# Attention, gated product and token mixing on one core: Newton steps of 1/sqrt and their transfers moved to GpSimd, stores of the w_out results issued by ScalarE, normalization moved behind the last gate, first attention by pairs of heads

## The chip, the core and the metric

One core of one Trainium2 chip runs the whole program. The core has TensorE (PE; its weight loads are shown as PEld), VectorE (DVE), ScalarE (ACT), GpSimd (POOL) and SyncE (SP), each with a queue of its own that it works off in order, and sixteen DMA engines which the queues of SP, ACT and POOL feed. The metric is the device time of the program in microseconds: 755.64 is the median of three runs of the kernel before.

## The reference, cut to what matters

```python
kv  = einsum('bhsd,bhse->bhde', k, v)              # 8 batches, 8 heads, 576 tokens, 64 wide
out = einsum('bhsd,bhde->bhse', q, kv)
x   = out / sqrt(mean(out * out, -1) + 1e-6) * g_norm   # per token and head, then heads side by side: 512 channels
g   = sigmoid(causal 5-tap convolution of x over the tokens, per channel)
x   = (g * (x @ w_val)) @ w_out                    # ends the first stage
theta = x @ w_theta                                # second stage
u   = x + w_tok_r @ (x * cos(theta)) + w_tok_i @ (x * sin(theta))
out = u + max(u @ w_ch, 0)
```

## The kernel before

Channels lie on the partitions, in four blocks of 128 (`m`), the 576 tokens on the free axis in two halves of 288. Every product with a weight is made of three fp32r matmuls (high times high, high times low part, low times high), so each operand is split: ScalarE rounds it (`xh`, `gh`, `wvh`, `woh`; L68), VectorE subtracts (`xl`, `gl`, ...; L69).

**First stage, per batch.** `key_value` makes keys times values for the 8 heads (TensorE, tile `kvp`; ScalarE copies it to `kvs`). `attention` makes four groups `o` of two heads' halves; of each, ScalarE takes the square (`sq`, L204) and a scaled copy into `x` (L205). Then 32 small matmuls (`ss`, L212) sum the squares; VectorE adds epsilon and makes 1/sqrt by an integer first guess and three Newton steps on 128x72 (L219 to L225, tiles `ss`, `hm`, `t`, `y`). For batches 2 to 7 `y` goes to DRAM (`rd`, L228) and comes back spread over all partitions (`yb`, L233), on SyncE's queue; for batches 0 and 1 TensorE spreads it by matmuls with `sel` into PSUM (`yb`, L254). `normalize` multiplies `x` by it (L246 from the transfer, L257 from PSUM) and splits `x`. `conv` makes the gate `acc`: ScalarE starts it (L263), VectorE adds four taps (L265), ScalarE takes the sigmoid (L266). `value` makes x times w_val for the four blocks (`v`); VectorE multiplies by the gate (L288, called the gate below) and the result is split into `gh` and `gl`. `first` makes the product with w_out (`y_0` to `y_3`): three quarters of y_0 and y_1, their last quarters (which need the fourth `gl`), then y_2 and y_3; ScalarE copies them (`yo`) and SyncE's queue stores them to DRAM (L305).

**The order.** The main loop over the batches is software pipelined: while batch i is in `value` and `first`, batch i+2 has its `key_value` and `attention`, and batch i+1 is normalized. All of a program's instructions are put on the engines' queues by a list scheduler, by priority in the order of the code and its own estimates, so code that moves is interleaved anew. `tc.issue_after(ins)` queues what a block puts on the engine of `ins` behind it. All products of the first stage share four PSUM slots of two banks (`pd`): `kvp`, `o`, `ss`, `yb`, `v` and `y` in turn, so a tile may wait until the tile before it in its slot has been read.

Weights come as 64 bit words and are decoded in four VectorE steps and one ScalarE step per chunk (`decode`), then split. The list START (L31) is the order of the first loads: v0 to v3 are chunks of w_val, o0 to o3 of w_out, k0 to k7 and q0 to q7 pairs of heads of batches 0 and 1, c0 the convolution. Decode of the second stage's weights (`todo`, `toks`; L429 to L440) is put behind the normalization of batches 1 to 6 at low priority.

**Second stage**: theta, the token mix `u` and the channel product `c`, batch after batch; the diff does not touch it.

Of the kernel before, what the change touches and what calls it, by code (L numbers as in the profile page):

```python
# [43 lines left out]
def attention_moe_holo_kernel(ctx, tc, kvm, kvt, qt, gn, w_val, conv_w, w_out, w_th, w_tok, w_ch, outT):  # L44
# [126 lines left out]
    def key_value(b, kv):  # L171

        ps = one_bank(f"kvp{b}")
        for g in range(2):
# [9 lines left out]
        kvs_of[b] = pa.tile([P, NP, D], F32, tag="kvs", bufs=2, name=f"kvs{b}")  # L184
        nc.scalar.activation(kvs_of[b], ps[:, 0:NP * D].rearrange("p (a e) -> p a e", e=D), AF.Copy)

    def attention(b, q):
# [5 lines left out]
        for h in range(2):  # L193
            sl = slice(h * HS, (h + 1) * HS)
            for g in range(2):
                o = two_banks(f"o{b}_{h}_{g}")
                for e in range(2):
                    for j in range(2):
                        rows = slice(j * D, (j + 1) * D)
                        mm = nc.tensor.matmul(o[e * D:(e + 1) * D, j, :], kv[rows, 2 * g + e, :], q[g][rows, e, sl],  # L200
                                              start=True, stop=True, tile_position=(j * D, e * D))
                ch = slice(2 * g, 2 * g + 2)
                sq[h, g] = px.tile([P, 2, HS], F32, tag="sq", bufs=4, name=f"sq{b}_{h}_{g}")
                nc.scalar.activation(sq[h, g], o, AF.Square, scale=0.125)  # L204
                nc.scalar.activation(x[:, ch, PAD + h * HS:PAD + (h + 1) * HS], o, AF.Copy, scale=gsb)  # L205
            yield x
# [12 lines left out]
        nc.vector.tensor_scalar(ss, sums, EPS, None, ALU.add)  # L219
        nc.vector.tensor_scalar(y.bitcast(I32), ss.bitcast(I32), -0.5, RSQRT_BITS, ALU.mult, ALU.add)  # L220
        nc.vector.tensor_scalar(hm, ss, -0.5, None, ALU.mult)
        for _ in range(3):
# [2 lines left out]
            nc.vector.scalar_tensor_tensor(y, t, 1.5, y, ALU.add, ALU.mult)  # L225
# [43 lines left out]
    def product(ps, w, m, xh, xl, t0, chunks=range(4)):  # L269
        tsl = slice(t0, t0 + HS)  # L270
        wh, wl = w
        for k in chunks:
# [3 lines left out]
            nc.tensor.matmul(ps, wh[:, m, ks], xl[:, k, tsl], start=False, stop=(k == 3))  # L276

    def value(b, x, xh, xl, sg, between):
        gh = pa.tile([P, NM, S], F32R, tag="gh", bufs=1, name=f"gh{b}")
        gl = pa.tile([P, NM, S], F32R, tag="gl", bufs=1, name=f"gl{b}")  # L280
        for m in range(NM):
            between(m)
            g = sg[m]
# [4 lines left out]
            nc.vector.tensor_tensor(halves(g), ps, halves(g), ALU.mult)  # L288
# [103 lines left out]
    for i in range(B):  # L392
# [217 lines left out]
```

## Time and profile before

| | us |
|---|---|
| median of three runs (lowest, highest) | 755.64 (752.99, 756.73) |
| the profiled execution, its own time | 753.31 |
| its span | 751.5 |
| first product of batch 0 (v_0) | 48.5 |
| first product of batch 1 / 5 / 7 | 89.6 / 224.2 / 286.1 |
| first mixing product of the second stage (u) | 330.5 |

The head of the page: busy time and share of the span, then the span in 40 slices of 18.8 us, each digit a busy share in tenths.

```profile
PE 709.7 (94%) x6000; PEld 669.9 (89%) x6000; DVE 523.9 (70%) x930; ACT 335.9 (45%) x560; POOL 20.7 (3%) x72
```

Rows of a timeline give start, length, engine, line, operation, written and read tiles, shapes, count, and in brackets the idle time of the engine before it and what ended it. A row of windows gives the window, its length, busy time and count of PE, PEld, DVE, ACT and POOL, TensorE's granted clock, the DMA share and GB/s.

### The profile page before, as it was taken

The numbers are of one execution on the slowest core, as the hardware profiler recorded it, in microseconds if no ns is written. First come the engines' busy times: TensorE is split into PE (matmuls) and PEld (weight loads), VectorE is DVE, ScalarE is ACT, GpSimd is POOL, SyncE is SP. The second block draws the span as 40 slices with busy tenths as digits, with TensorE's granted clock in tenths as the row PEclk, the third lists the DMA queues.
The fourth block names the chain that finished last, engine by engine and source line by source line (L and its number), as shares of the span: only waits on it lengthen the run. The fifth ranks groups of instructions, "written<-read, shape, count | busy, mean of one in ns | idle before, by whom it ended". The sixth has DMA issues, their size and how long they took to land.

```text
span 751.5 us, 14674 instructions
## 1 busy us (share of the span) xinstructions
PE 709.7 (94%) x6000; PEld 669.9 (89%) x6000; DVE 523.9 (70%) x930; ACT 335.9 (45%) x560; POOL 20.7 (3%) x72
## 2 busy tenths in 40 slices
PE   1679999999989999889999999999999999999998
PEld 1568999798987999879899899999999998998998
DVE  6389969798879999588983872853853835836504
ACT  2366565637464645376541640621622514514301
POOL 4000000000000000000000000000000000000000
PEclk9779999999999999999999999999999999999999
DMA  9948794979896358534345034163051270160101
GB/s 256 285 140 243 209 229 141 229 228 237 219 238 189 108 136 246 190 102 122 111 138 157 9 119 113 32 174 90 17 164 59 69 179 35 64 175 1 64 1 64
DMA packets 77059, 104.88 MB, mean 140 GB/s; under 512 B 11712, under 2 KB 42560, under 8 KB 76992
## 3 DMA queue, kind: packets, MB, share of 16 engines
q1 hardware_dynamic: 76416, 101.85, 48.5%
q0 software_dynamic: 576, 2.10, 0.9%
q8 instruction: 47, 0.77, 0.4%
q14 instruction: 20, 0.16, 0.1%
HBM read 72.73 MB, written 31.19 MB: 138 GB/s over the span
## 4 chain that ended last, share of the span: by engine, by line
PE 60%; DVE 24%; DMA 8%; ACT 4%; issue 3%; SPq 1%; POOL 0%; DVEq 0%; ACTq 0%; POOLq 0%
PE u L513 10%; PE u L511 10%; PE u L512 10%; DVE acc L265 10%; PE c L276 5%; PE c L274 5%; PE c L275 5%; DMA yb<-rd 4%; PE th L459 3%; PE th L457 3%; PE th L458 3%; DMA kv<-in_kvm_dram 2%; DVE x L246 2%; DVE xl L69 2%; DVE acc L288 2%
## 5 line engine op out<-in xcount | busy, mean ns | idle before, releaser
L516 DVE TENSOR_TENSOR f<-u,f 128x288 f32<-128x288 f32 x64 | 26.5, 455 | 129.8 <-PE u L513 129.8
L265 DVE SCALAR_TENSOR_TENSOR acc<-x,cw,acc 128x576 f32<-128x576 f32 x128 | 100.8, 817 | 1.3 <-ACT acc L263 1.3
L68 ACT ACTIVATE uh<-f 128x288 fp32r<-128x288 f32 x64 | 26.2, 444 | 152.4 <-DVE f L516 152.3
L274 PE MATMUL y<-gh,woh 128*128 128x288 f32 x256 | 77.8, 304 | 7.8 <-DVE acc L288 5.4
L274 PE MATMUL v<-xh,wvh 128*128 128x288 f32 x256 | 77.6, 303 | 0.7 <-DVE acc L288 0.7
L276 PE MATMUL v<-xl,wvh 128*128 128x288 f32 x256 | 76.5, 299 | 0.0
L276 PE MATMUL y<-gl,woh 128*128 128x288 f32 x256 | 75.8, 298 | 0.5 <-DVE gl L69 0.5
L275 PE MATMUL y<-gh,wol 128*128 128x288 f32 x256 | 76.0, 297 | 0.0
L275 PE MATMUL v<-xh,wvl 128*128 128x288 f32 x256 | 76.0, 297 | 0.0
L274 PE MATMUL c<-uh,wch 128*128 128x288 f32 x256 | 75.4, 295 | 0.0
L276 PE MATMUL c<-ul,wch 128*128 128x288 f32 x256 | 75.4, 295 | 0.0
L275 PE MATMUL c<-uh,wcl 128*128 128x288 f32 x256 | 75.4, 294 | 0.0
L274 PEld LDWEIGHTS y<-gh,woh 128*128 128x128 f32 x256 | 48.8, 191 | 11.9 <-DVE acc L288 6.1
L274 PEld LDWEIGHTS v<-xh,wvh 128*128 128x128 f32 x256 | 48.7, 190 | 4.6 <-issue 1.7
L459 PE MATMUL th<-wth,yl 128*128 128x512 f32 x128 | 50.3, 393 | 0.0
L458 PE MATMUL th<-wtl,yh 128*128 128x512 f32 x128 | 50.1, 391 | 0.0
L457 PE MATMUL th<-wth,yh 128*128 128x512 f32 x128 | 50.0, 391 | 0.0
L276 PEld LDWEIGHTS y<-gl,woh 128*128 128x128 f32 x256 | 48.4, 190 | 1.2 <-DVE gl L69 1.2
L276 PEld LDWEIGHTS v<-xl,wvh 128*128 128x128 f32 x256 | 48.6, 190 | 0.3 <-issue 0.2
L275 PEld LDWEIGHTS y<-gh,wol 128*128 128x128 f32 x256 | 48.8, 191 | 0.0
L275 PEld LDWEIGHTS v<-xh,wvl 128*128 128x128 f32 x256 | 48.7, 190 | 0.0
L275 PEld LDWEIGHTS c<-uh,wcl 128*128 128x128 f32 x256 | 48.0, 188 | 0.3
(188 smaller groups left out, 1946.0 us busy)
## 6 DMA issues: line engine op xcount, KB each, us to landing
kv<-in_kvm_dram SPq DMA_DIRECT2D x32, 512.0 KB, 8.6
q<-in_qt_dram SPq DMA_DIRECT2D x32, 288.0 KB, 8.9
yd<-yo SPq DMA_DIRECT2D x32, 288.0 KB, 2.4
f<-yd SPq DMA_DIRECT2D x32, 288.0 KB, 3.7
out_dram<-f SPq DMA_DIRECT2D x64, 144.0 KB, 1.8
sd<-fT SPq DMA_DIRECT2D x64, 128.0 KB, 2.5
yt<-sd SPq DMA_DIRECT2D x8, 1024.0 KB, 5.6
yb<-rd SPq DMA_DIRECT2D x12, 576.0 KB, 8.0
```

What stands on the lines that cost most here:

```text
L68: one = nc.scalar.activation(h, src, AF.Copy)
L265: nc.vector.scalar_tensor_tensor(a, x[:, m, k:k + S], cw[:, m * 5 + k:m * 5 + k + 1], a, ALU.mult, ALU.add)
L274: nc.tensor.matmul(ps, wh[:, m, ks], xh[:, k, tsl], start=(k == 0), stop=False)
L275: nc.tensor.matmul(ps, wl[:, m, ks], xh[:, k, tsl], start=False, stop=False)
L276: nc.tensor.matmul(ps, wh[:, m, ks], xl[:, k, tsl], start=False, stop=(k == 3))
L457: nc.tensor.matmul(ps, yh[:, k, :], wth[0][:, k, :], start=(k == 0), stop=False)
L458: nc.tensor.matmul(ps, yh[:, k, :], wth[1][:, k, :], start=False, stop=False)
L459: nc.tensor.matmul(ps, yl[:, k, :], wth[0][:, k, :], start=False, stop=(k == 3))
L511: nc.tensor.matmul(ps[:, :HS], zh[:, ms], wkh[:, j, sl], start=(i == 0), stop=False)
L512: nc.tensor.matmul(ps[:, :HS], zh[:, ms], wkl[:, j, sl], start=False, stop=False)
L513: nc.tensor.matmul(ps[:, :HS], zl[:, ms], wkh[:, j, sl], start=False, stop=(i == 8))
L516: nc.vector.tensor_tensor(f[:, m, sl], ps[:, :HS], f[:, m, sl], ALU.add)
```

## The change

Newton steps of batches 1 to 7 go from VectorE to GpSimd (the fused add-and-multiply becomes two instructions, on VectorE for batch 0 too); the sum with epsilon becomes a ScalarE copy; the store of the roots and their broadcast go from SyncE's queue to GpSimd's. The stores of `yo` go from SyncE's to ScalarE's queue. `normalize` of the next batch is queued behind the last split of the gated values (`gs[2][-1]`) on VectorE. The sums of the squares (`between()` in `first`) come between the three quarters and the last quarters of y_0 and y_1. Batch 0's attention runs pair of heads by pair of heads, with its scaled copies on VectorE; START loads the queries of batch 0 before the second w_val chunk; w_val chunks 1 to 3 are decoded behind the first normalization; key_value and attention of batch 1 move from before the first product into `value` of batch 0, those of batch 2 behind it.

```diff
-START = "v0 k0 k1 v1 k2 k3 v2 q0 q1 q2 q3 c0 v3 o0 k4 k5 k6 k7 o1 q4 q5 q6 q7 o2 o3"
-WVFIRST = 3
+START = "v0 k0 k1 q0 q1 k2 k3 q2 q3 v1 c0 v2 v3 k4 k5 k6 k7 o0 q4 q5 q6 q7 o1 o2 o3"
...
     def key_value(b, kv):
...
-        nc.scalar.activation(kvs_of[b], ps[:, 0:NP * D].rearrange("p (a e) -> p a e", e=D), AF.Copy)
+            if b == 0 or g == 1:
+                gs = slice(2 * g if b == 0 else 0, 2 * g + 2)
+                nc.scalar.activation(kvs_of[b][:, gs, :], ps[:, 0:NP * D].rearrange("p (a e) -> p a e", e=D)[:, gs], AF.Copy)
...
-        for h in range(2):
+        for n in range(4):
+            g, h = divmod(n, 2) if b == 0 else (n % 2, n // 2)
...
+            if b == 0:
+                nc.vector.tensor_scalar(xo, o, gsb, None, ALU.mult)
+            else:
+                nc.scalar.activation(xo, o, AF.Copy, scale=gsb)
...
-        nc.vector.tensor_scalar(ss, sums, EPS, None, ALU.add)
-        nc.vector.tensor_scalar(y.bitcast(I32), ss.bitcast(I32), -0.5, RSQRT_BITS, ALU.mult, ALU.add)
-        nc.vector.tensor_scalar(hm, ss, -0.5, None, ALU.mult)
+        if b == 0:
+            nc.vector.tensor_scalar(ss, sums, EPS, None, ALU.add)
+        else:
+            nc.scalar.activation(ss, sums, AF.Copy, bias=EPS)
+        eng = nc.vector if b == 0 else nc.gpsimd
+        eng.tensor_scalar(y.bitcast(I32), ss.bitcast(I32), -0.5, RSQRT_BITS, ALU.mult, ALU.add)
+        eng.tensor_scalar(hm, ss, -0.5, None, ALU.mult)
         for _ in range(3):
-            nc.vector.tensor_tensor(t, y, y, ALU.mult)
-            nc.vector.tensor_tensor(t, t, hm, ALU.mult)
-            nc.vector.scalar_tensor_tensor(y, t, 1.5, y, ALU.add, ALU.mult)
+            eng.tensor_tensor(t, y, y, ALU.mult)
+            eng.tensor_tensor(t, t, hm, ALU.mult)
+            eng.tensor_scalar(t, t, 1.5, None, ALU.add)
+            eng.tensor_tensor(y, t, y, ALU.mult)
         if b >= SPREAD:
-            nc.sync.dma_start(out=rdram[b], in_=y)
+            nc.gpsimd.dma_start(out=rdram[b], in_=y)
...
-                nc.sync.dma_start(out=yb[i * D:(i + 1) * D], in_=rows)
+                nc.gpsimd.dma_start(out=yb[i * D:(i + 1) * D], in_=rows)
...
-                nc.sync.dma_start(out=ydram[b][:, m, :], in_=yo)
+                nc.scalar.dma_start(out=ydram[b][:, m, :], in_=yo)
...
         part(0, range(3))
         part(1, range(3))
+        between()
         part(0, (3,))
         part(1, (3,))
-        between()
...
     key_value(0, kvs.pop(0))
-    for k in range(WVFIRST):
-        weight_chunk(px, wv, w_val, k, "wv", raw=raw[f"v{k}"])
+    weight_chunk(px, wv, w_val, 0, "wv", raw=raw["v0"])
+    *_, xy = attention(0, qs)
+    *_, (xs, last) = normalize(0, *xy)
     nc.vector.tensor_copy(cw, decode(px, raw["c0"], NM * 5, "cw", "c"))
-    *_, xy = attention(0, qs.pop(0))
-    *_, (xs, last) = normalize(0, *xy)
-    key_value(1, kvs.pop(1))
-    *_, xy = attention(1, qs.pop(1))
-    sg = [conv(0, m, xs[0]) for m in range(EARLY)]
-    with tc.issue_after(last.ins):
-        for n in range(WVFIRST, 4):
+    sg = []
+    for n in range(1, NM):
+        with tc.issue_after(last.ins):
             weight_chunk(px, wv, w_val, n, "wv", raw=raw[f"v{n}"])
-    kvs[2], qs[2] = load_kv(2), load_q(2)
+        if n <= EARLY:
+            sg.append(conv(0, n - 1, xs[0]))
...
+            if i == 0 and m == 2:
+                with tc.issue_after(done.ins):
+                    key_value(1, kvs.pop(1))
...
+        second = attention(1, qs) if i == 0 else None
         gs = value(i, *xs, sg, between)
+        if i == 0:
+            *_, xy = second
+            kvs[2], qs[2] = load_kv(2), load_q(2)
+            key_value(2, kvs.pop(2))
+            kvs[3] = load_kv(3)
+            next(ahead)
...
         if i + 1 < B:
-            *_, (nxs, last) = normalize(i + 1, *xy)
+            with tc.issue_after(gs[2][-1].ins):
+                *_, (nxs, last) = normalize(i + 1, *xy)
         if i == 0:
-            for k in range(4):
-                weight_chunk(px, wo, w_out, k, "wo", raw=raw[f"o{k}"])
+            with tc.issue_after(gs[2][1].ins):
+                for k in range(4):
+                    weight_chunk(px, wo, w_out, k, "wo", raw=raw[f"o{k}"])
```

Where instructions stand, before and after, at three places. **VectorE, end of `value` of batch 1**; L246 (L257 after) normalizes batch 2, `acc_3` is the last gate, `wt` a chunk of w_theta. Before:

```order
L69 TENSOR_TENSOR gl_1066<-acc_2_1095,gh_1065 128x576
L246 TENSOR_TENSOR x_740<-x_740,yb_992 128x4x288 x2
L94 TENSOR_SCALAR dst_wt_1481<-raw_wt_1479 128x512
L288 TENSOR_TENSOR acc_3_1189<-v_3_1242,acc_3_1189 128x576
L95 SCALAR_TENSOR_TENSOR dst_wt_1481<-raw_wt_1479,dst_wt_1481 128x512
L69 TENSOR_TENSOR xl_1293<-x_740,xh_1292 128x4x288
L69 TENSOR_TENSOR gl_1066<-acc_3_1189,gh_1065 128x576
```

After:

```order
L68 TENSOR_TENSOR gl_1076<-acc_2_1105,gh_1075 128x576
L301 TENSOR_TENSOR acc_3_1199<-v_3_1252,acc_3_1199 128x576
L68 TENSOR_TENSOR gl_1076<-acc_3_1199,gh_1075 128x576
L257 TENSOR_TENSOR x_775<-x_775,yb_984 128x4x288 x2
L93 TENSOR_SCALAR dst_wt_1494<-raw_wt_1492 128x512
L68 TENSOR_TENSOR xl_1303<-x_775,xh_1302 128x4x288 x2
```

The gate and its gl now stand ahead of the normalization. **GpSimd, roots of batch 2 in batch 0's `first`**; `kv` and `x` are the cleared edges of later tiles. Before:

```order
L155 MEMSET kv_3_673 64x2x128
L191 MEMSET x_1224 128x4x4
L155 MEMSET kv_0_1145 64x2x128
L155 MEMSET kv_1_1149 64x2x128
L155 MEMSET kv_2_1153 64x2x128
```

After, with the last five of the 14 steps:

```order
L236 TENSOR_TENSOR y_965<-t_966,y_965 128x72
L233 TENSOR_TENSOR t_966<-y_965 128x72
L234 TENSOR_TENSOR t_966<-t_966,hm_967 128x72
L235 TENSOR_SCALAR t_966<-t_966 128x72
L236 TENSOR_TENSOR y_965<-t_966,y_965 128x72
L239 DMA rd_80<-y_965 128x72
L244 DMA yb_984<-rd_80 64x4x576 x2
L192 MEMSET x_1234 128x4x4
L154 MEMSET kv_0_1155 64x2x128
```

The steps and both transfers stand in GpSimd's queue, ahead of the clearing of the next key tiles. **ScalarE, attention of batch 0**; `kvs` is the copy of keys times values, `cw` the convolution's weights. Before:

```order
L185 ACTIVATE kvs_249<-kvp_208 128x256
L204 ACTIVATE sq_0_0_289<-o_0_0_284 128x576
L204 ACTIVATE sq_0_1_297<-o_0_1_292 128x576
L205 ACTIVATE x_282<-o_0_0_284,gsb 128x2x288
L97 ACTIVATE raw_cw<-raw_cw 128x20
L205 ACTIVATE x_282<-o_0_1_292,gsb 128x2x288
L204 ACTIVATE sq_1_0_305<-o_1_0_300 128x576
L205 ACTIVATE x_282<-o_1_0_300,gsb 128x2x288
L204 ACTIVATE sq_1_1_313<-o_1_1_308 128x576
```

After:

```order
L186 ACTIVATE kvs_209<-kvp_208 128x128
L206 ACTIVATE sq_0_0_267<-o_0_0_262 128x576
L206 ACTIVATE sq_1_0_275<-o_1_0_270 128x576
L186 ACTIVATE kvs_209<-kvp_208 128x128
L206 ACTIVATE sq_0_1_283<-o_0_1_278 128x576
L96 ACTIVATE raw_cw<-raw_cw 128x20
L206 ACTIVATE sq_1_1_291<-o_1_1_286 128x576
```

Two of the four squares stand ahead of the second half of keys times values, and the copies into `x` are gone from this queue. In TensorE's queue the spreading of batch 1's roots (`yb`) stands directly ahead of y_0 of batch 0, before and after.

More of the change, by code (lines that the diff above doesn't have):

```diff
@@ L173, in key_value @@
         ps = one_bank(f"kvp{b}")
+        kvs_of[b] = pa.tile([P, NP, D], F32, tag="kvs", bufs=2, name=f"kvs{b}")
         for g in range(2):
@@ L192, in attention @@
         sq = {}
-        for h in range(2):
+        for n in range(4):
+            g, h = divmod(n, 2) if b == 0 else (n % 2, n // 2)
             sl = slice(h * HS, (h + 1) * HS)
[L195 to L206, printed above, removed]
+            o = two_banks(f"o{b}_{h}_{g}")
+            for e in range(2):
+                for j in range(2):
+                    rows = slice(j * D, (j + 1) * D)
+                    nc.tensor.matmul(o[e * D:(e + 1) * D, j, :], kv[rows, 2 * g + e, :], q[g][rows, e, sl],
+                                     start=True, stop=True, tile_position=(j * D, e * D))
+            xo = x[:, 2 * g:2 * g + 2, PAD + h * HS:PAD + (h + 1) * HS]
+            sq[h, g] = px.tile([P, 2, HS], F32, tag="sq", bufs=4, name=f"sq{b}_{h}_{g}")
+            nc.scalar.activation(sq[h, g], o, AF.Square, scale=0.125)
+            if b == 0:
+                nc.vector.tensor_scalar(xo, o, gsb, None, ALU.mult)
+            else:
+                nc.scalar.activation(xo, o, AF.Copy, scale=gsb)
+            if n % 2:
+                yield x
         sums = one_bank(f"ss{b}")[:, :TB]
@@ L280, in value @@
         gl = pa.tile([P, NM, S], F32R, tag="gl", bufs=1, name=f"gl{b}")
+        lasts, done = [], None
         for m in range(NM):
-            between(m)
+            between(m, done)
             g = sg[m]
@@ L362, in attention_moe_holo_kernel @@
     raw = {}
+    nc.scalar.dma_start(out=gsb[0:D], in_=gn)
+    nc.scalar.dma_start(out=gsb[D:P], in_=gn)
     for what in START.split():
@@ L401, in attention_moe_holo_kernel, with between @@
         if two:
-            ahead = attention(i + 2, qs.pop(i + 2))
-        def between(m):
-            if two and m == 1:
+            ahead = attention(i + 2, qs)
+        def between(m, done):
+            if i == 0 and m == 2:
+                with tc.issue_after(done.ins):
+                    key_value(1, kvs.pop(1))
+            if two and i and m == 1:
                 key_value(i + 2, kvs.pop(i + 2))
@@ L410, in between @@
             if two and m == 3:
-                next(ahead)
+                next(ahead if i else second)
+        second = attention(1, qs) if i == 0 else None
         gs = value(i, *xs, sg, between)
+        if i == 0:
[4 more added lines that the diff above has]
+            next(ahead)
         if two:
@@ L418, in attention_moe_holo_kernel @@
         if i + 1 < B:
[L419 removed]
+            with tc.issue_after(gs[2][-1].ins):
+                *_, (nxs, last) = normalize(i + 1, *xy)
         if i == 0:
[L421 to L422 removed]
+            with tc.issue_after(gs[2][1].ins):
+                for k in range(4):
+                    weight_chunk(px, wo, w_out, k, "wo", raw=raw[f"o{k}"])
         got = []
[L424 removed]
+        first(i, *gs[:2], lambda: got.append(next(ahead) if two else None))
         xy = got[-1]
@@ L430, in attention_moe_holo_kernel @@
             with tc.high_priority(offset=-LATER), tc.issue_after(last.ins):
-                for _ in range(RATE[0] if i < 6 else 8):
+                for _ in range(RATE[0]):
                     if todo:
@@ L434, in attention_moe_holo_kernel @@
                         weight_chunk(px, w, src, k, name, scale)
-                for _ in range(RATE[1] if i < 6 else 11):
+                for _ in range(RATE[1]):
                     if toks:
```

17 lines of the change are left out of this document (7 added, 10 removed).

## The prediction

> **What bounds the kernel now.** I read the page first, then the product stage batch by batch, then the waits of TensorE. The second stage is left alone (the diff ends before it), so the 33.5 us per batch of the first stage and the way into it are what can move. These rows are windows cut at the first value product of each of the eight batches: length, then busy time of PE, PEld, DVE, ACT, POOL.
>
> ```profile
> 48.53:89.56 41.03, 40.92 (x467) 36.63 (x465) 38.10 (x73) 24.72 (x40) 1.51 (x5) 0.94 0.74 199
> 89.56:121.65 32.09, 32.09 (x370) 30.04 (x369) 25.95 (x44) 18.18 (x28) 1.18 (x5) 1.00 0.73 187
> 121.65:155.88 34.23, 32.71 (x371) 30.12 (x369) 29.61 (x51) 19.48 (x30) 1.19 (x5) 1.00 0.85 220
> 155.88:189.06 33.18, 32.40 (x371) 29.95 (x369) 29.96 (x51) 19.40 (x31) 1.80 (x5) 1.00 0.84 224
> 189.06:224.19 35.13, 32.42 (x371) 30.07 (x370) 27.73 (x49) 17.99 (x29) 1.45 (x5) 1.00 0.89 223
> 224.19:258.91 34.72, 32.71 (x371) 29.97 (x370) 34.37 (x61) 21.39 (x34) 0.39 (x1) 1.00 0.52 159
> 258.91:286.11 27.20, 25.96 (x194) 25.49 (x193) 25.66 (x44) 14.17 (x23) 0.00 (x0) 1.00 0.51 146
> ```
>
> Batch 1 runs without a hole: 32.09 us is TensorE's own pace. Batches 2 to 5 have the same matmuls and take 2.14, 1.09, 3.04 and 2.63 us more, batch 6 has 1.24 us of holes. Together 10.1 us: all that the steady part can give back. Who makes the holes (waiter, releaser: total us, times, longest):
>
> ```profile
> PE y L274 <- DVE acc L288: 5.4, 3, 2.5
> PE yb L254 <- DVE y L225: 3.1, 1, 3.1
> PE y L274 <- ACT x L205: 1.4, 4, 0.5
> PE o L200 <- ACT x L205: 1.2, 2, 0.9
> PE y L274 <- ACT gh L68: 1.0, 1, 1.0
> ```
>
> The first is no slow gate. VectorE's timeline in batch 2 shows it held up by what stands before the gate:
>
> ```profile
> 140.20 2.63 DVE L246 TENSOR_TENSOR x<-x,yb 128x1152 f32<-128x1152 f32 x2 [1.89 <-DMA yb<-rd]
> 142.75 0.75 DVE L288 TENSOR_TENSOR acc<-v,acc 128x576 f32<-128x576 f32 x1
> 143.41 2.62 DVE L69 TENSOR_TENSOR xl<-x,xh 128x1152 fp32r<-128x1152 f32 x2
> 145.95 0.76 DVE L69 TENSOR_TENSOR gl<-acc,gh 128x576 fp32r<-128x576 f32 x1
> ```
>
> L246 (normalization of the next batch) waits for the broadcast of the roots, and the last gate stands behind it, though TensorE wants the gate's bank for y_1 at once.
>
> **Steady part, batches 1 to 6.** Normalization goes behind the last gate and its gl; the sums matmuls of the batch after next go between three quarters of y_0, y_1 and their last quarter, where they cover 1.1 us of the wait for gl; ScalarE takes xh behind the last gh and the last attention groups. So the DVE row above and the three ACT rows lose their cause. What is late next is VectorE itself. Its prices:
>
> ```profile
> 41.66 4.46 DVE L265 SCALAR_TENSOR_TENSOR acc<-x,cw,acc 128x576 f32<-128x576 f32 x6
> 120.70 0.82 DVE L265 SCALAR_TENSOR_TENSOR acc<-x,cw,acc 128x576 f32<-128x576 f32 x1
> 121.43 0.24 DVE L225 SCALAR_TENSOR_TENSOR y<-t,y 128x72 f32<-128x72 f32 x1
> 121.58 0.82 DVE L265 SCALAR_TENSOR_TENSOR acc<-x,cw,acc 128x576 f32<-128x576 f32 x1
> 13.18 0.69 DVE L98 SCALAR_TENSOR_TENSOR dst_wv<-raw_wv,dst_wv 128x512 f32<-128x512 f32 x1
> 13.78 0.69 DVE L95 SCALAR_TENSOR_TENSOR dst_wv<-raw_wv,dst_wv 128x512 int32<-128x512 int32 x1
> ```
>
> A convolution step costs 0.73 us in a row (4.46 for six); with one Newton step between, two starts lie 0.88 apart, so a step costs 0.15, and the twelve that leave give back 1.8 us per batch. A decode step is 0.60. One batch then needs 16 x 0.73 + 8 x 0.67 (gates, gl) + 4 x 1.27 (L246, xl) = 22.1 us, plus decode of the later weights: counted in the new order, 8.0 us in batch 2, 7.0, 6.2, and 10.0 in batch 5.
>
> **Newton on GpSimd** is what no row shows. Fourteen dependent steps of 128x72 (the fused step becomes two). One step lies between a 128x1 memset and a 64x256 one:
>
> ```profile
> 4.05 0.09 POOL L120 MEMSET halfpi<- 128x1 f32 x1
> 2.54 0.31 POOL L155 MEMSET kv<- 64x256 f32 x1
> 4.21 4.02 POOL L147 TENSOR_SCALAR_AFFINE_SELECT sel<-sel 32x1024 f32<-32x1024 f32 x3
> 5.69 1.52 DVE L95 SCALAR_TENSOR_TENSOR dst_wv<-raw_wv,dst_wv 128x512 int32<-128x512 int32 x1
> 11.51 0.69 DVE L95 SCALAR_TENSOR_TENSOR dst_wv<-raw_wv,dst_wv 128x512 int32<-128x512 int32 x1
> ```
>
> So 1.3 to 4.3 us for the chain alone; I take 0.2 each, 2.8. But the last two rows matter more: the same VectorE step took 1.52 us while GpSimd ran L147, which reads SBUF, and 0.69 after it had ended. The two took turns. The Trainium skill, page "SBUF — State Buffer", section "Who interferes with whom", says the like: a VectorE instruction with two SBUF inputs and a GpSimd instruction that reads SBUF exclude each other for their whole length. The trace agrees with it. I therefore take turns as the likeliest: each of the 14 steps waits for one VectorE step of 0.60 to 0.73 and holds up the next one for 0.2. The chain lasts 14 x 0.85 = 12 us (before, woven into VectorE's queue, about 10), and VectorE loses 2.8 us for the 1.8 it was given.
>
> VectorE per batch: 22.1 + decode + 2.8 + 0.9 (waits for gh): 33.8 in batch 2, 32.8, 32.0, 35.8 in batch 5, against 32.09 of TensorE. It may lag some 2.8 us before y_1 misses its bank (o groups 1.1 and half of y_0 2.4 lie between, less the gate's 0.67). The lags of batches 2 to 4 fit in about that, batch 5 sticks out by some 2. Steady part: 10.1 - 2 = **8 us gained**. The roots may come later than before, but they are wanted later too (behind gl): nothing. The stores of y leave SyncE's queue, where key loads stood behind them, and go to ScalarE's: the loads already land ahead of their use (no wait of PE for them after the start), so nothing is gained. The two rates that are dropped after batch 5 moved nothing: four weight chunks at 1 and eleven pieces at 3 per batch are used up in batch 4. ScalarE's four added DMA issues, and the sum's copy, go into an engine busy 18 to 21 us of 33: nothing; if that cover went, four issues of the store row's 0.3 us are 1.3 us of ScalarE.
>
> **Start and batch 0.** The loads are a stream at full rate; the first product stands where attention of batch 1 lets it.
>
> ```profile
> 0.00:20.00 20.00, 3.96 (x54) 3.40 (x56) 11.30 (x15) 5.40 (x8) 9.22 (x36) 1.00 0.94 254
> raw_wv<-in_w_val_dram SPq DMA_DIRECT2D x4, 512.0 KB, 6.3
> q<-in_qt_dram SPq DMA_DIRECT2D x32, 288.0 KB, 8.9
> 8.55 10.79 DMA kv<-in_kvm_dram
> 23.43 0.65 ACT L204 ACTIVATE sq<-o 128x576 f32<-128x576 f32 x1 [1.23 <-PE o L200]
> 27.49 0.68 ACT L204 ACTIVATE sq<-o 128x576 f32<-128x576 f32 x1
> 37.00 1.36 DVE L69 TENSOR_TENSOR xl<-x,xh 128x1152 fp32r<-128x1152 f32 x1 [0.30 <-ACT xh L68]
> 48.53 0.61 PE L274 MATMUL v<-xh,wvh 128*128 128x288 f32 x1
> 71.69 3.77 PE L254 MATMUL yb<-y,sel 32*128 32x72 f32 x64
> ```
>
> (The first row is the window of the first 20 us, its last number GB/s; then two DMA rows, KB each; then the chain that ended last, ScalarE, VectorE and TensorE.) The last key tile, which landed at 19.34 before, loses two weight chunks ahead of it (1.05 MB) and gains two of the four query transfers (0.59 MB): 0.46 MB at 254 GB/s, 1.8 us. After it two squares are left instead of four squares and three copies (4.7 us from 23.43 to 28.17, now 1.65): 3.1 us. Three more Newton steps: -0.65. So xl's first half, 38.35 before, stands at 34.1, and v_0 follows at once: 14 us sooner than 48.53. That is not the gain. VectorE then has, in its new order, 16 convolutions, xl, decode of six chunks (about 2.7 each, 0.6 of the last missing), four gates, four gl: 34.2 us, until 68.9. The third gate, whose bank the sums of batch 1 take, ends 23.5 us into that, at 58.2; with ScalarE's squares, sums and copy, Newton of batch 1 begins at 61.2. TensorE can't go round it: its queue has yb of batch 1 ahead of y_0. With turns Newton ends at 73, yb (3.77) at 76.8. Before, y_0 began where yb ended, at 75.46. So the 14 us are eaten and **1.4 us are lost**. The bounds: alone Newton takes 1.3 to 4.3 us, and the banks that yb needs (ScalarE's copies of batch 2, then L268) let y_0 begin at 71.8, a gain of 3.6; with turns of a full 0.73 + 0.31 it ends at 75.8 and y_0 begins at 79.6, a loss of 4.1.
>
> **Sum.** 8 - 1.4 = 6.7 us off the span of 751.5 (the profiled execution took 753.31, 1.8 around its span, and lies 2.3 below the median of the runs). From the median: 755.64 - 6.7 = **749 us**.
>
> **Rivals.**
> *No turns.* GpSimd runs beside VectorE. Then 3.6 at the start and all 10.1: 742 us. For it: the steps are short and write 288 bytes a partition; against: the row of 1.52.
> *A wash.* VectorE becomes the bound where decode is, and TensorE, which idles from about 66 to 72 in batch 0, comes back at the lower clock. A window like that is in the trace:
>
> ```profile
> 20.00:48.53 28.53, 18.58 (x336) 15.28 (x332) 17.25 (x36) 15.00 (x25) 1.67 (x6) 0.79 0.94 261
> ```
>
> With pauses of some us TensorE had 0.79 of its clock there, and 1.00 in batch 1. Half speed over yb and the first 4 us of y_0 is 1.9 + 2. "TensorE: Matmul & The Clock Gate" of the Trainium skill, Part 1, has the array throttled after an idle window of about 3.4 us, which by it would happen here. Start -5, steady part 10.1 - 5: 755 us. That is also the case in which the waits only change their name (y for gl instead of y for the bank).
> *Slower.* The roots' round trip becomes the loop. The store of the roots to DRAM, and the time to landing of their broadcast (tile yb):
>
> ```profile
> rd<-y SPq DMA_DIRECT2D x6, 36.0 KB, 1.5
> DMA to landing us min/median/max: 5.7/8.0/11.2
> ```
>
> Sum copy, Newton (14 at worst), store (1.5 and its issue 0.7), broadcast from GpSimd's queue beside the next key tiles (11.2 at worst), then L246, xh and the four accumulator starts that stand ahead of the next sum copy on ScalarE, about 7: 34.7 us per batch against 32.09. It decides from a Newton-to-broadcast time of 25 us on. Batch 1 then loses 2.6, batches 2 to 5 (137.3 before, 138.8 then) 1.5, the start 4.5, batch 6 gains 1.2: 763 us.
>
> **Chances.** Forecast 0.46 (its own range 745 to 753), no turns 0.17, wash 0.20, slower 0.17. The range 740 to 760 leaves out the far half of the last and the tail of the second. A measurement of this kernel tells 0.5% (3.8 us) from no change: faster 0.60 (no turns and nearly all of the forecast), same 0.23, slower 0.17.
>
> **What would show it.** Right: GpSimd's steps spread to 0.8 us apart while VectorE's convolutions stretch by 0.2; no wait of y for the gate L301 in batches 2 to 4, batch 5 still over 33 us; y_0 of batch 0 at 75 to 78 behind yb. Wrong: Newton in 4 us and y_0 at 72 (then 742), or L257 waiting for yb in every batch (then 763).

## The result, and the profile after

The changed kernel takes 775.30 us (median of 4 runs, 773.10 to 776.12) beside 754.60 for the kernel before (4 runs, 752.99 to 756.73): ratio 1.0268, 95% interval 1.0231 to 1.0304, so it is slower. The profiled execution has a span of 771.3 us, 19.8 more than before. The medians of e6, e10 and e12 below are of three runs each, without one slow run (777.45, 891.03 and 773.48 us). These are the windows of the changed kernel, cut at the first value product of each batch like those of before:

```profile
35.30:94.75 59.45, 51.51 (x608) 43.97 (x609) 56.13 (x82) 36.26 (x58) 17.45 (x24) 0.89 0.75 201
94.75:127.38 32.63, 32.38 (x371) 30.10 (x369) 17.81 (x23) 16.05 (x25) 12.80 (x27) 1.00 0.65 174
127.38:163.68 36.30, 32.73 (x371) 29.98 (x369) 31.14 (x44) 21.37 (x34) 12.50 (x23) 1.00 0.76 223
163.68:199.56 35.88, 32.73 (x370) 29.98 (x369) 30.48 (x42) 19.85 (x32) 12.79 (x23) 1.00 0.76 225
199.56:237.29 37.73, 34.02 (x370) 31.48 (x369) 31.22 (x43) 20.49 (x33) 14.11 (x25) 0.95 0.75 215
237.29:278.75 41.46, 35.09 (x371) 31.78 (x370) 33.91 (x48) 21.93 (x36) 12.54 (x19) 0.88 0.33 105
278.75:304.18 25.43, 25.43 (x195) 25.43 (x193) 20.51 (x28) 10.65 (x16) 6.87 (x11) 1.00 0.63 187
```

v_0 is early (35.3 instead of 48.5), and nothing is left of that at batch 1, which starts at 94.75 instead of 89.56. Batches 1 to 5 take 184.0 us instead of 169.4: here are 14.6 of the 19.8 us. TensorE's holes were to go; they have grown. In batches 4 and 5 the granted clock is lower too (0.95, 0.88), and TensorE is busy 34.0 and 35.1 us there where it was 32.4 and 32.7 before: some 4 of the 14.6 us. VectorE is busy 30 to 34 us of 36 to 41 in batches 2 to 5, so it idles too. Its waits in batches 1 to 6 (waiter, releaser: total us, times, longest), then TensorE's:

```profile
DVE dst_tk L93 <- DMA raw_tk<-in_w_tok_dram: 9.7, 3, 4.2
DVE gl L68 <- ACT gh L67: 8.7, 11, 0.8
DVE acc L301 <- PE v L287: 8.2, 4, 3.5
DVE x L257 <- DMA yb<-rd: 7.5, 3, 3.4
DVE dst_tk L93 <- DMA td<-dst_tk: 7.0, 1, 7.0
...
PE o L202 <- DVE acc L301: 5.7, 1, 5.7
PE y L285 <- ACT ss L228: 4.6, 4, 3.3
PE v L285 <- DVE acc L301: 3.1, 2, 1.6
```

The largest, 16.7 us in two rows, are of a step that the prediction counted only as busy time: L93, the first step of decoding a piece of the token weights (`tk`) or a chunk of w_theta (`wt`), waits for the piece's fetch (`raw_tk`) or for a store (`td`) that must read the buffer it wants to write. VectorE's and SyncE's timelines in batch 2:

```profile
147.01 0.75 DVE L301 TENSOR_TENSOR acc<-v,acc 128x576 f32<-128x576 f32 x1
152.00 0.43 DVE L93 TENSOR_SCALAR dst_tk<-raw_tk 128x512 int32<-128x512 int32 x1 [4.24 <-DMA raw_tk<-in_w_tok_dram]
152.47 0.69 DVE L94 SCALAR_TENSOR_TENSOR dst_tk<-raw_tk,dst_tk 128x512 int32<-128x512 int32 x1
153.08 0.75 DVE L68 TENSOR_TENSOR gl<-acc,gh 128x576 fp32r<-128x576 f32 x1
153.74 1.35 DVE L257 TENSOR_TENSOR x<-x,yb 128x1152 f32<-128x1152 f32 x1
...
141.28 3.93 SPq L463 DMA_DIRECT2D td<-dst_tk  x2
145.31 0.38 SPq L84 DMA_DIRECT2D raw_tk<-in_w_tok_dram  x1
```

The fetch is issued at 145.31 and asked for from 147.76 on; until it lands, the last `gl` and the normalization stand behind L93.

### The profile page after: what moved, and what is told of

It is laid out like the page before. It is cut to its first block, busy times and chain, and to the rows that moved or that the text cites. A ratio compares the mean times of both kernels' runs of the same rounds, so it can differ in the third digit from the quotient of the medians.

```text
span 771.3 us, 14690 instructions
## 1 busy us (share of the span) xinstructions
PE 720.1 (93%) x6000; PEld 675.3 (88%) x6000; DVE 520.9 (68%) x853; ACT 336.2 (44%) x564; POOL 100.8 (13%) x188
## 4 chain that ended last, share of the span: by engine, by line
PE 60%; DVE 18%; DMA 10%; POOL 4%; ACT 4%; issue 3%; SPq 0%; ACTq 0%; DVEq 0%; POOLq 0%
PE u L536 10%; PE u L534 10%; PE u L535 10%; DVE acc L276 7%; PE c L287 4%; PE c L286 4%; PE c L285 4%; DMA yb<-rd 4%; PE th L482 3%; PE th L480 3%; PE th L481 3%; DMA kv<-in_kvm_dram 2%; DVE x L257 2%; DMA raw_tk<-in_w_tok_dram 2%; DVE xl L68 1%
## 5 line engine op out<-in xcount | busy, mean ns | idle before, releaser
L276 DVE SCALAR_TENSOR_TENSOR acc<-x,cw,acc 128x576 f32<-128x576 f32 x128 | 99.1, 837 | 0.9 <-ACT acc L274 0.8
L285 PE MATMUL y<-gh,woh 128*128 128x288 f32 x256 | 80.7, 316 | 8.4 <-ACT ss L228 4.6
L286 PE MATMUL y<-gh,wol 128*128 128x288 f32 x256 | 78.4, 307 | 0.0
L287 PE MATMUL y<-gl,woh 128*128 128x288 f32 x256 | 78.0, 307 | 0.4 <-DVE gl L68 0.4
L285 PEld LDWEIGHTS y<-gh,woh 128*128 128x128 f32 x256 | 51.4, 201 | 13.2 <-ACT ss L228 5.5
L287 PEld LDWEIGHTS y<-gl,woh 128*128 128x128 f32 x256 | 50.9, 200 | 0.6 <-DVE gl L68 0.6
L286 PEld LDWEIGHTS y<-gh,wol 128*128 128x128 f32 x256 | 51.2, 200 | 0.0
```

What stands on the lines that cost most here:

```text
L276: nc.vector.scalar_tensor_tensor(a, x[:, m, k:k + S], cw[:, m * 5 + k:m * 5 + k + 1], a, ALU.mult, ALU.add)
L285: nc.tensor.matmul(ps, wh[:, m, ks], xh[:, k, tsl], start=(k == 0), stop=False)
L286: nc.tensor.matmul(ps, wl[:, m, ks], xh[:, k, tsl], start=False, stop=False)
L287: done = nc.tensor.matmul(ps, wh[:, m, ks], xl[:, k, tsl], start=False, stop=(k == 3))
```

## The experiments

Boundaries of batches in these runs are cut as above; "the steady part" is batches 1 to 5 (169.4 us before, 184.0 after). Unless said otherwise the edit is to the changed kernel.

**The parts of the change.** e3 undoes Newton and its transfers; e4 and e7 put one part on the kernel before; e8 is e3 with the stores of y on SyncE's queue again.

e3:

```diff
-        eng = nc.vector if b == 0 else nc.gpsimd
+        eng = nc.vector
...
-            eng.tensor_scalar(t, t, 1.5, None, ALU.add)
-            eng.tensor_tensor(y, t, y, ALU.mult)
+            eng.scalar_tensor_tensor(y, t, 1.5, y, ALU.add, ALU.mult)
...
-            nc.gpsimd.dma_start(out=rdram[b], in_=y)
+            nc.sync.dma_start(out=rdram[b], in_=y)
```

(the broadcast likewise, and the sum's copy on VectorE for all batches)

> After the change, but Newton, the sum's copy and the transfers of the roots undone (VectorE, fused steps, SyncE); start, order of normalization, and the y stores stay. Both theories want most back here: D because the decode's third piece falls into the next batch again (no L93 ahead of the last gl), R because the roots' way is short. Steady part under 33.5 us per batch: 752 to 758. If it stays above 765, the start or the y stores on ScalarE's queue make the loss, and neither theory holds.

e4, to the kernel before (with `lasts` kept in `value`, as in the change):

```diff
+        between()
         part(0, (3,))
         part(1, (3,))
-        between()
...
-            *_, (nxs, last) = normalize(i + 1, *xy)
+            with tc.issue_after(gs[2][-1].ins):
+                *_, (nxs, last) = normalize(i + 1, *xy)
```

> Before the change, with only the order in a batch changed: normalization behind the last gate, the sums' matmuls before the last quarters of y_0 and y_1. The prediction's steady part: VectorE's wait at the last gate is gone, 8 us gained: 744 to 749. Rival: the wait for yb only changes its place, from the last gate to the next batch's first products: 752 to 757.

e7, to the kernel before: e3's edits the other way round.

> Before the change, with only Newton, the sum's copy and the transfers of the roots moved to GpSimd (and ScalarE). VectorE's order then has L246 (normalization, L251 here) between the first gate and the first gl's successors, three gates earlier than before, where it waits for the broadcast. Theory D in its wider form (what Newton's move costs is what it does to VectorE's order): slower than after, 785 us or more, with PE waiting for gates behind L251. Theory R: the same 20 us as in after against e3, 770 to 778. If Newton on GpSimd is harmless in itself and needs no order: 745 to 756.

e8, to e3: `nc.scalar.dma_start` of `ydram` becomes `nc.sync.dma_start`.

> As e3 (Newton, sum's copy and transfers undone), and the stores of y issued by SyncE again. The prediction held them at nothing: within 3 us of e3's 748. If ScalarE's own waits for its stores (8.7 us of L313 for yd in e3) count, this is 3 us or more faster; if SyncE's queue is what the roots' store needs free, 3 us or more slower.

| | us | ratio to before (95%) | steady part |
|---|---|---|---|
| e3, all but Newton and transfers | 747.79 | 0.9924 (0.9899 to 0.9949) | 161.6 |
| e4, before with the order in a batch alone | 749.26 | 0.9962 (0.9935 to 0.9988) | 161.9 |
| e7, before with Newton's move alone | 826.62 | 1.0981 (1.0902 to 1.1061) | 232.4 |
| e8, as e3, y stores on SyncE | 747.13 | 0.9927 (0.9902 to 0.9952) | 161.6 |

Two windows of e3, batches 2 and 4, show the loop at TensorE's own pace but for one small hole:

```profile
125.15:157.26 32.11, 32.11 (x370) 30.06 (x369) 31.03 (x54) 18.98 (x30) 1.23 (x5) 1.00 0.84 242
189.37:222.37 33.00, 32.46 (x370) 29.94 (x369) 30.37 (x54) 18.93 (x29) 1.24 (x5) 1.00 0.84 236
```

So in the steady part the order in a batch gives the 8 us that were predicted (7.8 in e3, 7.4 in e4); of the whole time, by the ratios, 5.7 and 2.9 us are left. The start gives or takes too little to be seen beside it (e3 against e4), the stores' queue nothing; Newton's move takes all of that and 20 us more. In e7, on the old order, it takes 73: the scheduler there puts the normalization ahead of the second gate (not three gates earlier than before, as the expectation has it, but two), where VectorE waits for the roots:

```profile
DVE x L251 <- DMA yb<-rd: 71.2, 5, 16.1
```

**Why does Newton's move cost that?** Theory D says by VectorE's order and the decoding in it; theory R by the roots' way being too long for the loop.

e1:

```diff
-RATE = (1, 3)
+RATE = (1, 2)
```

> After the change, but with two pieces of the token weights decoded per batch instead of three (batches 1 to 6 take 2 x 6 = 12 for the 11 pieces), so that the three raw buffers hold a batch's whole lot and no fetch stands behind a td store. Theory D (decode: VectorE stands before the last gl in L93, waiting for a fetch that SyncE's queue issues late): VectorE's waits of L93 for raw_tk (9.7 us) and td (7.0) fall under 2 us together, batches 2, 3 and 5 shorten by 2 to 5 us each, batch 6 gains 1 to 2: 763 to 767 us. Theory R (roots: the way Newton, store, broadcast through GpSimd's queue has become the loop): the roots come no sooner, L257 still waits some 7 us for yb: over 771.

e2: `nc.gpsimd.dma_start` of `rd` and `yb` become `nc.sync.dma_start`, Newton stays.

> After the change, but the store of the roots and their broadcast issued by SyncE again; Newton stays on GpSimd. Theory R: rd lands in 1.5 us instead of 6, L257's waits for yb (7.5 us in all) go below 2, and 4 to 8 us come back: 767 to 771. Theory D: VectorE's order around the last gl is the same row by row, its L93 still waits 15 us or more, and the time stays within 3 us of 775.

e5:

```diff
-        if 1 <= i < B - 1:
+        if i == B - 2:
...
-                for _ in range(RATE[0]):
+                for _ in range(4):
...
-                for _ in range(RATE[1]):
+                for _ in range(11):
```

> After the change, Newton on GpSimd kept, but all decoding of the later weights (4 chunks, 11 pieces) put behind batch 6, so that batches 1 to 5 have none; the whole run is longer by the decoding that now stands alone and only the batches are compared. Theory D (decode in VectorE's order, waiting for late fetches, makes the steady loss): batches 2 to 5, 36.3, 35.9, 37.7 and 41.5 before this edit, run at 32.1 to 33 us each. Theory R (the roots' way, or turns with GpSimd, are too slow for the loop by themselves): they stay at 34.5 us or more, with L257 waiting for yb.

e1 took 764.73 us (1.0162, 1.0102 to 1.0222): 8 us came back by the ratios, as theory D had it. Its steady part is 170.9 us, 13.1 less, though batches 3 and 5 still take 37 us; TensorE then waits 11.1 us for token weights (`wkh`) ahead of the second stage's first u, since their decoding now ends later. e2 took 777.75 (1.0327, 1.0281 to 1.0373): the roots' broadcast is issued 1.5 us behind their store again and VectorE's order is that of the changed kernel step by step, but nothing came back. The steady part is 191.4 us. VectorE hardly waits for the roots any more, and 25.5 us in L93:

```profile
DVE dst_tk L93 <- DMA raw_tk<-in_w_tok_dram: 15.9, 2, 8.4
DVE dst_wt L93 <- DMA td<-dst_tk: 9.6, 1, 9.6
...
DVE x L257 <- DMA yb<-rd: 0.4, 1, 0.4
```

e5's steady part is 162.8 us, with Newton on GpSimd (the whole run, 793.84 us, has all the decoding behind it); batch 3 and VectorE's wait for the roots there:

```profile
160.43:192.66 32.23, 32.23 (x370) 30.08 (x369) 23.35 (x29) 17.70 (x28) 12.96 (x23) 1.00 0.69 186
...
DVE x L257 <- DMA yb<-rd: 13.7, 4, 4.0
```

Here is what decides: VectorE waits 13.7 us for the roots, and the steady part is 1.2 us longer than e3's. Newton's move, late roots included, fits into the loop without the decoding, and so does the decoding without the move (e3). Together they don't, and not because the roots are late: in e2 they are there in time, with as great a loss. What is left is the decoding, in the order that VectorE has with the move.

**What in the decoding?** e6 holds the third piece back behind the next L257; e9 adds VectorE's old eleven Newton steps as a dead computation; e10 and e11 take the td stores off SyncE's queue; e12 gives the fetches a fourth buffer.

e6 (`store_piece` decodes and stores; the held piece comes first in the next lot):

```diff
+                while held:
+                    store_piece(*held.pop())
...
-                        nc.sync.dma_start(out=tokdram[:, sl], in_=decode(px, raw, sl.stop - sl.start, f"tk_{j}"))
+                        if n == 2:
+                            held.append((j, raw))
+                        else:
+                            store_piece(j, raw)
```

> After the change, Newton on GpSimd kept, and the same four pieces per batch, but the third token piece of each lot is decoded behind the next batch's normalization (L257) instead of where there is room in VectorE's order. Theory D: L93 no longer stands ahead of the last gl; waits of L93 for raw_tk and td in batches 2 to 5 fall by more than half, batches 2 and 3 at 32 to 34 us, the whole at 755 to 766. If it stays over 772 the place ahead of the last gl is not what costs.

e9:

```diff
+        if b:
+            y2, t2, hm2 = [px.tile([P, TB], F32, tag=n, bufs=2, name=f"{n}_{b}") for n in ("y2", "t2", "hm2")]
+            nc.vector.tensor_scalar(y2.bitcast(I32), ss.bitcast(I32), -0.5, RSQRT_BITS, ALU.mult, ALU.add)
+            nc.vector.tensor_scalar(hm2, ss, -0.5, None, ALU.mult)
+            for _ in range(3):
+                nc.vector.tensor_tensor(t2, y2, y2, ALU.mult)
+                nc.vector.tensor_tensor(t2, t2, hm2, ALU.mult)
+                nc.vector.scalar_tensor_tensor(y2, t2, 1.5, y2, ALU.add, ALU.mult)
```

> After the change, Newton on GpSimd kept, and VectorE does its old eleven steps as well, into tiles that nobody reads, so that its load is as before. It tells two reasons apart why VectorE's decoding comes earlier in its order. If the lighter load of VectorE made room for it: the decoding goes back, batches 2 to 5 at 32 to 33.5 us, about 750 us. If it is the roots, which come later from GpSimd than from VectorE and leave room ahead of the normalization: the order keeps L93 ahead of the last gl (as its rows show), the waits of L93 for its fetches stay near the 17 us of after, and the time is 775 us or more.

e10, and the like with `nc.gpsimd` for e11:

```diff
-                        nc.sync.dma_start(out=tokdram[:, sl], in_=decode(px, raw, sl.stop - sl.start, f"tk_{j}"))
+                        nc.scalar.dma_start(out=tokdram[:, sl], in_=decode(px, raw, sl.stop - sl.start, f"tk_{j}"))
```

> After the change, but the decoded token weights are stored by ScalarE's queue, so that SyncE's fetches no longer stand behind a store that waits for VectorE. Theory D, and in it the queue: the third piece's fetch goes out when its raw buffer is free, some 6 us sooner (139 instead of 145.3 in batch 2), L93's waits for raw_tk and td fall from 17 us to under 6, batches 2 to 5 shorten by 8 us or more together: 760 to 767 us. If the buffers (three) and not the queue hold the fetch, or ScalarE now waits for L97 in VectorE's place, it stays within 4 us of 775.

> As e10, with GpSimd's queue instead of ScalarE's: the fetches are as free as there, but Newton stands behind stores that wait for VectorE. Fetch waits under 6 us as in e10; if GpSimd's queue matters, L257 waits for yb 10 us or more and the time is above e10's by 5 us; else within 4 us of e10.

e12:

```diff
-            raw = pool.tile([P, width if tag else DM, words], I32, tag="raw" + tag, bufs=1 if tag else 3, name=f"raw_{name}")
+            raw = pool.tile([P, width if tag else DM, words], I32, tag="raw" + tag, bufs=1 if tag else 4, name=f"raw_{name}")
...
-        t = px.tile([P, TB], F32, tag="t", bufs=2, name=f"t{b}")
-        hm = px.tile([P, TB], F32, tag="hm", bufs=2, name=f"hm{b}")
+        t = px.tile([P, TB], F32, tag="t", bufs=1, name=f"t{b}")
+        hm = px.tile([P, TB], F32, tag="hm", bufs=1, name=f"hm{b}")
```

> After the change, Newton and the transfers on GpSimd, but with four raw buffers for the weights' pieces instead of three (room made by single buffers for t and hm), so that a lot's four fetches are issued ahead of the next key loads; VectorE's order keeps the third piece's decoding early, ahead even of the last gate. Theory D as it stands after e10 (the fetch comes late, behind 2.4 MB of key loads in SyncE's queue and in the DMA engines, and the decoding that asks for it stands early in VectorE's order): L93's waits for raw_tk and td fall from 17 us to under 3, batches 2 to 5 run at 32 to 33.5 us as in e5, 750 to 757 us. If the place of the decoding by itself costs (its steps ahead of gates), batches 2 to 4 stay over 34.5 us without waits of L93, 762 us or more.

No cure brought more than some 8 us by the ratios. e6: 767.89 (1.0196, 1.0134 to 1.0258); e10: 777.18 (1.0341, 1.0297 to 1.0384); e11: 777.63 in one run; e12: 768.76 (1.0167, 1.0099 to 1.0235). e6's trace, of its run of 777.45 us, has 14.5 us of L93 waiting for raw_tk. The held piece itself doesn't wait any more, but in batches 3 and 4 another piece waits ahead of the last gate:

```profile
187.96 0.43 DVE L93 TENSOR_SCALAR dst_tk<-raw_tk 128x512 int32<-128x512 int32 x1 [6.72 <-DMA raw_tk<-in_w_tok_dram]
188.42 0.69 DVE L94 SCALAR_TENSOR_TENSOR dst_tk<-raw_tk,dst_tk 128x512 int32<-128x512 int32 x1
189.03 0.75 DVE L301 TENSOR_TENSOR acc<-v,acc 128x576 f32<-128x576 f32 x1
```

So e6 doesn't test what it was meant to, decoding with nothing of it ahead of the last gate. e9: 782.93 in one run, with L93 waiting up to 8.3 us ahead of the last gate, so it isn't VectorE's lighter load that lets the decoding come forward. That it is the roots' later time, by the scheduler's own estimates, is what is left of the two, and was only argued. In e10 the fetch is issued as late in its batch as before, 17.7 us behind its start, now held by the key loads ahead of it, and VectorE, which asks for it ahead of the last gate, waits longer. In e12 no wait for a fetch is left in VectorE's list, and the next one in the line has taken its place. First e10's row in batch 2, then e12's wait and its batch 2:

```profile
149.85 0.43 DVE L93 TENSOR_SCALAR dst_tk<-raw_tk 128x512 int32<-128x512 int32 x1 [7.88 <-DMA raw_tk<-in_w_tok_dram]
...
DVE dst_tk L93 <- DMA td<-dst_tk: 11.3, 2, 6.7
...
127.21:162.70 35.49, 32.46 (x370) 29.95 (x369) 33.38 (x47) 20.93 (x34) 13.85 (x25) 1.00 0.85 245
```

e12's batch 2 has no wait of L93 at all and is still 3.4 us too long: the decoding of one chunk and three pieces (47 VectorE instructions in that batch, 33.4 us) doesn't fit between normalization and last gate. So the waits and the place of the decoding both cost, and a cure of one wait alone shows the next.

**Both taken away: e13 to e16.** e13 decodes one chunk and two pieces per batch (three pieces from batch 5 on) instead of one and three, behind the convolution of the next batch's second channel block instead of behind its normalization; e14 is the same with Newton on VectorE; e15 and e16 bring parts of the move back.

```diff
-            nc.vector.scalar_tensor_tensor(a, x[:, m, k:k + S], cw[:, m * 5 + k:m * 5 + k + 1], a, ALU.mult, ALU.add)
+            sig[b, m] = nc.vector.scalar_tensor_tensor(a, x[:, m, k:k + S], cw[:, m * 5 + k:m * 5 + k + 1], a, ALU.mult, ALU.add)
...
-            with tc.high_priority(offset=-LATER), tc.issue_after(last.ins):
+            with tc.high_priority(offset=-LATER), tc.issue_after(sig[i + 1, 1].ins):
...
-                for _ in range(RATE[1]):
+                for _ in range(2 if i < 5 else 3):
```

> After the change, Newton and the transfers on GpSimd, but VectorE's decoding is paced: two token pieces and one chunk per batch (three pieces from batch 5 on), placed behind the last convolution step of the next batch's second channel block instead of behind its normalization, so that the fetches have half a batch of lead and nothing of it stands ahead of the last two gates. Theory D: L93's waits under 2 us in batches 1 to 5, which run at 32.1 to 33.2 us each as in e5, the whole 747 to 755 us: what Newton's move cost was the place of the decoding. If Newton on GpSimd costs something itself (turns, roots): 34 us or more per batch with L257 waiting for yb, 762 us or more.

> As e13 with Newton, sum's copy and transfers back on VectorE and SyncE. Beside e13 it gives the price of Newton's place alone, at the same pace of decoding: theory D says under 4 us between the two, 745 to 750 us here. If e13 is 10 us or more above it, the place of the decoding isn't all.

> As e13 (paced decoding, Newton on GpSimd), with the roots' store and broadcast issued by SyncE. VectorE's order is that of e13 row by row, so nothing but the roots' way changes. The 13 us between e13 and e14 are the roots' way (23 us from the sums' last matmul to the broadcast's issue in after, 11 in e14: Newton 2 us longer, the store to DRAM 5.5, the sum's copy 5): then L257's waits for yb (7.1 us in e13) fall under 3 and the time to 751 to 756. If it stays at 757 or more, the transfers aren't it, as e2 said of after.

> As e15, with the sum's copy on VectorE as before, so that only the Newton steps themselves are on GpSimd. If the copy's place behind xh and the accumulator starts on ScalarE (5 us, and y_2's bank with it) matters: 746 to 751, within 4 us of e14. If the steps on GpSimd themselves are the cost, it stays at e15's time, 753 or more.

| paced decoding, with | us | ratio to before (95%) | steady part |
|---|---|---|---|
| e13: Newton, copy and transfers as changed | 758.58 | 1.0067 (1.0041 to 1.0093) | 168.8 |
| e15: transfers on SyncE | 754.39 | 1.0007 (0.9983 to 1.0031) | 162.5 |
| e16: and the sum's copy on VectorE | 754.71 | 1.0000 (0.9982 to 1.0018) | 162.9 |
| e14: and the steps on VectorE | 745.41 | 0.9900 (0.9866 to 0.9935) | 160.8 |

Pacing, rate and place together, gives back 15 of the 26 us (by the ratios) between the changed kernel and e3; in the steady part, the rate alone had given 13.1 us in e1 where e13 gives 15.2. The difference between e13 and e14 is 13 us, more than the 4 that theory D allowed: 4 us for the transfers, nothing that can be told for the copy, 8 to 9 with the steps. VectorE's wait in e13, gone in e15, and batch 3 in e15 and e14:

```profile
DVE x L257 <- DMA yb<-rd: 7.1, 3, 4.0
...
158.39:191.06 32.67, 32.21 (x371) 29.98 (x370) 30.63 (x42) 20.00 (x32) 11.64 (x20) 1.00 0.85 243
...
154.87:187.04 32.17, 32.17 (x370) 30.07 (x369) 31.11 (x55) 20.02 (x31) 1.23 (x5) 1.00 0.87 246
```

Of the 7.2 us between the spans of e15 (750.2) and e14 (743.0), 3.1 are there when batch 1 starts (93.62 against 90.57, of which v_0 makes 1.1), 1.7 come in batches 1 to 5 and 2.4 in batches 6 and 7. There the decoding's place costs once more: in batch 6 VectorE waits 4.0 us in L93 for a td store and TensorE 3.8 us for the `gl` behind it, in e15 and not in e14. The starts of single executions differ by as much (v_0 of e4, which has the order of before up to there, came at 52.5, before at 48.5), so what of the 8 to 9 us is Newton's chain in the start stays open. e14 is the fastest kernel of the study, 1% below the kernel before.

## Why the prediction was wrong, point by point

**Steady part: the step that failed.** "Steady part: 10.1 - 2 = **8 us gained**" rests on VectorE's sum, in which decoding stands as busy time alone ("counted in the new order, 8.0 us in batch 2, 7.0, 6.2, and 10.0 in batch 5"). That decoding could wait, for its fetches or for its stores, was put at nothing without a reason: the one sentence on loads, "the loads already land ahead of their use", speaks of key loads and was read from TensorE's waits in the kernel before. But use is where the order puts it, and in the changed kernel the third piece's first step stands ahead of the last `gl` (152.00 and 153.08 above). e3's two rows for the same fetch and use show what VectorE's order has without Newton's move:

```profile
146.68 0.33 SPq L84 DMA_DIRECT2D raw_tk<-in_w_tok_dram  x1
...
160.72 0.41 DVE L93 TENSOR_SCALAR dst_tk<-raw_tk 128x512 int32<-128x512 int32 x1
```

14 us lie between issue and use there, 2.4 in the changed kernel (145.31, 147.76). The waits of L93, 16.7 us in all, were missing from the sum, and so was that decoding ahead of the last gates delays them even without a wait (e12). The steady part is 14.6 us lost instead of 8 gained. Without Newton's move (e3) the order in a batch does give what the prediction took for it, 7.8 us, and without the decoding (e5) 6.6. Why the scheduler brings the decoding forward with the move stays open.

**"The roots may come later than before, but they are wanted later too (behind gl): nothing."** True of the loop without decoding (e5: 1.2 us), and in the changed kernel earlier roots bring nothing (e2). Wrong once the decoding is paced: with equal VectorE order the transfers alone cost 4 us (e15 against e13). How late the roots are, and by what, shows in the changed kernel's ScalarE, GpSimd and its queue behind batch 1's sums (TensorE's first row), and in SyncE's queue in e14:

```profile
117.65 1.21 PE L218 MATMUL ss<-sq,ind 128*32 128x72 f32 x64
...
118.82 2.43 ACT L67 ACTIVATE xh<-x 128x1152 fp32r<-128x1152 f32 x2 [3.27 <-DVE x L257]
121.16 2.76 ACT L274 ACTIVATE acc<-x,cw 128x576 f32<-128x576 f32 x4
123.82 0.21 ACT L228 ACTIVATE ss<-ss 128x72 f32<-128x72 f32 x1
...
124.21 0.28 POOL L230 TENSOR_SCALAR y<-ss 128x72 int32<-128x72 int32 x1 [12.67 <-ACT ss L228]
134.04 0.60 POOL L236 TENSOR_TENSOR y<-t,y 128x72 f32<-128x72 f32 x1
134.93 0.64 POOL L239 DMA_DIRECT2D rd<-y  x1 [0.30 <-POOL y L236]
141.97 0.63 POOL L244 DMA_DIRECT2D yb<-rd  x1 [6.40 <-DVE dst_tk L93]
...
125.50 0.33 SPq L235 DMA_DIRECT2D rd<-y  x1
127.01 1.25 SPq L240 DMA_DIRECT2D yb<-rd  x2
```

From the sums' end (118.86) to the broadcast's issue it is 23.1 us: 5.0 until ScalarE, which has xh and the accumulator starts ahead of it, comes to the copy, 11.1 for it and Newton, 7.0 from the store's issue to the broadcast's. In e14 the last part is 1.5. The rival "slower" had this chain, with 14 us for Newton and 2.2 for the store, and put its turning point at 25 us. As the cause of this loss it falls with e2 and e5; the 4 us of the paced kernels are what is left of it.

**Turns between GpSimd and VectorE: right in the main.** From the first step's start to the last one's it is 9.8 us for 13 distances, 0.76 each (0.85 predicted). VectorE's price was mis-sized: a convolution was to lose 0.2 us per turn; in these rows of e13 and e14 (busy us, then mean ns) the mean of all is 34 ns longer, and inside a chain some 50 (0.78 from start to start instead of 0.73):

```profile
L276 DVE SCALAR_TENSOR_TENSOR acc<-x,cw,acc 128x576 f32<-128x576 f32 x102 | 78.7, 842 | 2.3 <-ACT acc L274 2.3
...
L272 DVE SCALAR_TENSOR_TENSOR acc<-x,cw,acc 128x576 f32<-128x576 f32 x104 | 82.8, 808 | 0.7 <-ACT acc L270 0.7
```

So VectorE did gain, 1.8 us less some 0.6 per batch. TensorE had no use for it: its pace bounds the loop in e3 already.

**Start.** v_0 came at 35.3 (34.1 predicted), Newton of batch 1 began at 64.5 (61.2), the yb matmuls ended and y_0 began at 79.2 (76.8), for the reason given: TensorE's queue has yb of batch 1 ahead of y_0. Newton took 9.8 us there instead of 12, but yb 4.9 instead of the 3.77 that the forecast took over from before: the granted clock was 0.61 from 74.4 to 79.2 us, and 1.00 over yb before. That is what the rival "a wash" had for this place. The loss, 3.8 us against the one profile of before, is within what the start varies: with the order of before, y_0 began at 78.3 in e4.

**Stores of y, and the sum's copy: "nothing".** Right for the stores (e8 against e3), and for the copy where the decoding is paced (e16 against e15); in the changed kernel the copy, late on ScalarE, holds y_2's bank for 4.6 us in the waits above. The two dropped rates weren't tried.

**What was to show it.** "batch 5 still over 33 us" and "no wait of y for the gate L301 in batches 2 to 4" came true in the letter (41.5 us; the waits there are of `o` and `v`, and of y for ScalarE's copy L228), which shows how little such signs say if a sum lacks a term. "L257 waiting for yb in every batch (then 763)" came in three batches, and the time was above that. y_0 of batch 0, looked for "at 75 to 78 behind yb", came at 79.2.

## What to carry to other kernels

When a change takes work off an engine whose order a scheduler makes, read in the new order which waiting instructions move ahead of the gates of the critical loop, and set each one's place against the time at which its load is issued and lands. Try the parts together as well as alone: Newton's move without the decoding (e5) and the decoding without the move (e3) each fitted into the loop, and together they cost 21 us of the steady part. If a wait's cure only makes room for the next wait (e6, e10, e12), change the pace or the place of the waiting work, not its loads.

## What the runs showed of the hardware that was not expected

The store of the roots, 36 KB, took 1.5 us from issue to landing on SyncE's queue and 5.6 on GpSimd's (medians of six, e15 and the changed kernel):

```profile
rd<-y POOLq DMA_DIRECT2D x6, 36.0 KB, 5.6
...
rd<-y SPq DMA_DIRECT2D x6, 36.0 KB, 1.5
```

On GpSimd's queue four of the six took 5.3 to 6.5 us and the last two 1.9. What in GpSimd's queue takes the 4 us wasn't tried. The turns are uneven, too: a Newton step on GpSimd takes 0.38 to 0.48 us from start to start where VectorE leaves it alone, and 0.66 to 0.88 beside convolutions, which lose only 0.05. One step in batch 0 stood 8.69 us, until 95.83, while VectorE ran thirteen convolution steps without a gap, until 96.57. The Trainium skill, page "SBUF — State Buffer", section "Who interferes with whom", has the two kinds exclude each other, which fits this row. In the other chains they alternate, and no run here shows why this step found no turn:

```profile
87.14 8.69 POOL L230 TENSOR_SCALAR y<-ss 128x72 int32<-128x72 int32 x1 [12.79 <-ACT ss L228]
...
86.87 9.70 DVE L276 SCALAR_TENSOR_TENSOR acc<-x,cw,acc 128x576 f32<-128x576 f32 x13
```
